# Attention scores in one fp32 product, with the queries read from DRAM onto diagonal blocks

## The chip, the cores and the metric

The kernel runs on one core of one Trainium2 chip. The core has five engines that run side by side and meet through semaphores: TensorE (PE, with its weight load shown apart as PEld), VectorE (DVE), ScalarE (ACT), GpSimd (POOL) and SyncE (SP), which here only issues DMAs. The metric is the device time of one execution in microseconds; lower is better.

## The reference, cut to what matters

A gated linear attention over 768 steps for 4 batches of 8 heads with 40 dimensions feeds a mixture of 8 experts (top 1) and then a dense two-layer network. Only the first part is touched:

```python
for t in range(S):
    m_new = np.maximum(f_gate[:, :, t] + m, i_gate[:, :, t])
    f_stab = np.exp(f_gate[:, :, t] + m - m_new)
    i_stab = np.exp(i_gate[:, :, t] - m_new)
    m = m_new
    C = f_stab * C + i_stab * np.einsum('bhd,bhe->bhde', vt, kt)
    n = f_stab * n + i_stab * kt
    h_tilde = np.einsum('bhde,bhe->bhd', C, qt)
    denom = np.maximum(np.abs(np.einsum('bhd,bhd->bh', n, qt)), 1.0)
    y[:, :, t] = sigmoid(o_gate[:, :, t]) * h_tilde / denom
x = moe(y)          # expert by argmax of x @ w_gate
return ffn(x)       # leaky relu between two dense products
```

## The kernel before

The attention is computed in chunks of 128 steps: 6 chunks, and in each the 32 heads in 11 groups of three (the last has two). One chunk and one group is an **item**; there are 66, and I count them from 1. All of this is the first stage, up to some 228 us; the experts and the dense network come after it and are not changed.

Per item `e_decay` makes the matrix E of gate decays (one product pD of `down` with the gate rows `GM`, then three exponentials on ScalarE). `e_scores` makes pS, the products of 128 keys with 128 queries of each of the three heads: the 120 stacked key rows of the group are the weights, and the queries stand on diagonal blocks of a 120 x 384 tile `qB` whose other blocks are zero, so that one product gives three separate score matrices. VectorE multiplies P = E * pS (L574). `e_out` (L600 to L612) multiplies P, the carried state Cm and the weighted keys kw; `e_kw`, Cm and sums of hA run on POOL.

pS is exact to fp32 by three products of rounded parts: `parts` splits queries and keys of a piece into a high and a low fp32r part (ScalarE casts L539 and L546, VectorE subtracts L542 and L549). A piece is three groups (the last has two), so a chunk has 4 and the stage 24. `blocks` (L333) then copies the rounded queries, high and low side by side, from `qs` in SBUF onto the diagonal blocks of `qB` by three DMAs a piece on SP's queue. There are two `qB` tiles, used in turn.

The order is written out by hand. The loop goes by steps s: step s issues the scores of item s, then the outputs of the item before, and at three points of each step (`small`) whatever a table (`later`) has put there; key 3*s+k is point k of step s. Each engine and SP's queue take their instructions in the order in which they are written. The tables: PART_AT and PO place the splits; GATES the gate sums of chunks 1 to 5; Z0, ZS the 16 writes of zeros (L843) to the rows `xs_d` that are later scattered to the experts; PICK, FR, W1S, TW the first expert's choice, its rows, its weights and the last rows. Short products of a constant tile `rest` (L261) fill known waits of TensorE.

Of the kernel before, what the change touches and what calls it, by code (L numbers as in the profile page):

```python
# [9 lines left out]
F32 = mybir.dt.float32  # L10
# [41 lines left out]
def tile_mlstm_moe_ffn(  # L52
# [189 lines left out]
    with ExitStack() as sx:  # L242
# [37 lines left out]
        QB = [s1.tile([GR, GW, HG, 2, P], F32R, tag=f"qB{i}", name=f"qB{i}") for i in range(2)]  # L280
        for t in QB:
            nc.gpsimd.memset(t.bitcast(F32), 0.0)
# [46 lines left out]
        def blocks(src, dst, p):  # L329
            for j in range(HG):  # L330
                r = slice(D * j, D * j + D)
                nj = sum(HG * g + j < BH for g in range(GCUT[p], GCUT[p + 1]))
                nc.sync.dma_start(dst[r, 0:nj, j].bitcast(F32), src[r, 0:nj].bitcast(F32))  # L333

        def first_loads(p):
            gs = slice(GCUT[p], GCUT[p + 1])
            nc.sync.dma_start(nats["Q", 0][:, gs], qt[0, :, gs])
            nc.sync.dma_start(nats["K", 0][:, gs], kt[0, :, gs])

# [13 lines left out]
        for w in "QKkv":  # L353
            new_nat(w, 0)
# [47 lines left out]
        def gate_steps(c0, c1, eng):  # L402
# [42 lines left out]
            def decays(k):  # L445
# [63 lines left out]
        LD0, LDS, LD1 = 16, 0, -1  # L509
        XO = (11, 14, 2, 10), (7, 14, 0, 10), (9, 14, 1, 10), (7, 10, 4, 9), (9, 14, 1, 10), (6, 10, 0, 11)  # L510
        PART_AT = -15, -8, -8, -4, -5
        PO = 0, 0, 1, 0, 0, 0, 0, 0, 0, 1, 0, 0, 0, 0, 0, 0, 0, 0, 0, 0, 0, 0, 0, 1
        ZC = 2
        Z0, ZS = 24, 1
        TA, TB = 3, 3
        GATES = 1, 3, 8, 9, 10, 11, 12, 18, 20, 22, 23, 25, 27, 28
# [6 lines left out]
        SC0 = 49  # L523
# [3 lines left out]
        def q_blocks(n):  # L527
            c, g = items[n]
            p = piece_of(g)
            return QB[(c * NP + p) % 2][:, g - GCUT[p]]  # L530

        def parts(c, p, k):

            gs = slice(GCUT[p], GCUT[p + 1])
            n = GCUT[p + 1] - GCUT[p]
            kt_, qt_ = (nats[w, c][:, gs] for w in "KQ")
            if k == 0:
                qs = st["qs", c, p] = wk.tile([GR, GW, 2, L], F32R, tag="qs", name=f"qs{c}_{p}")
                nc.scalar.copy(qs[:, :n, 0], qt_)  # L539
            if k == 1:  # L540
                qs = st["qs", c, p]
                nc.vector.tensor_tensor(qs[:, :n, 1], qt_, qs[:, :n, 0].bitcast(F32), ALU.subtract)  # L542
            if k == 2:
                kh, kl = (wk.tile([GR, GW, L], F32R, tag=w, name=f"{w}{c}_{p}") for w in ("kh", "kl"))
                st["k", c, p] = kh, kl
                nc.scalar.copy(kh[:, :n], kt_)  # L546
            if k == 3:
                kh, kl = st["k", c, p]
                nc.vector.tensor_tensor(kl[:, :n], kt_, kh[:, :n].bitcast(F32), ALU.subtract)  # L549
            if k == 4:  # L550
                qs = st.pop(("qs", c, p))
                blocks(qs, QB[(c * NP + p) % 2], p)

# [306 lines left out]
        g_row(0, slice(0, BH))  # L860
        for i in (0, 1, 4, 2, 3):
# [780 lines left out]
```

## Time and profile before

| what | us |
|---|---|
| median of 3 runs (817.66 to 819.74) | 819.6 |
| profiled execution, its own time | 821.43 |
| span of its trace | 819.6 |
| TensorE busy in the span | 754.8 |
| VectorE busy | 503.8 |
| ScalarE busy | 378.0 |
| GpSimd busy | 272.8 |

[...] Matmul records overlap, so the pace of TensorE is read from the distance between starts rather than from durations.

### The profile page before, as it was taken

Reading aid. Unit: us, or ns where it says so; the run is one execution under the profiler, and the core shown is the slowest. Engines: PE = TensorE matmul, PEld = TensorE weight load, DVE = VectorE, ACT = ScalarE, POOL = GpSimd, SP = SyncE. Lnnn points to the kernel's source line nnn. Section 1 sums busy time; section 2 is a strip of 40 time slices with the busy share of each in tenths; the row PEclk is TensorE's granted clock in tenths of the full one; section 3 lists DMA queues with packets and bytes.
Section 4 is the critical chain, followed back from the end, with each engine's and each line's share of the span. In section 5 each row is a group of like instructions: output and inputs, shape, how many; then the busy total and the mean of one; then the engine's idle time right before and its main releaser. Section 6 shows DMA issues by size and latency. Waiting matters only on the chain.

```text
span 819.6 us, 12632 instructions
## 1 busy us (share of the span) xinstructions
PE 754.8 (92%) x4332; PEld 680.9 (83%) x4332; DVE 503.8 (61%) x1097; ACT 378.0 (46%) x842; POOL 272.8 (33%) x434
## 2 busy tenths in 40 slices
PE   5888898897988999989898999999999999999992
PEld 2678898897876788979787999899999999999992
DVE  7485898785576887865866478554443444444330
ACT  5575776463145565544554345433343343343330
POOL 5343776652643355454445332300200200201002
PEclk7899999996799999999898999999999999999996
DMA  5699565633246457777784931100000000000000
GB/s 152 197 330 251 158 212 163 210 116 107 97 135 190 138 177 186 146 195 195 166 198 156 242 124 37 65 1 1 33 1 1 33 1 0 33 1 17 17 1 34
DMA packets 60936, 92.57 MB, mean 113 GB/s; under 512 B 9508, under 2 KB 41508, under 8 KB 60868
## 3 DMA queue, kind: packets, MB, share of 16 engines
q1 hardware_dynamic: 45508, 61.28, 28.0%
q10 hardware_dynamic: 9344, 18.35, 7.2%
q0 software_dynamic: 6016, 12.09, 4.9%
q8 instruction: 36, 0.59, 0.3%
q14 instruction: 32, 0.26, 0.1%
HBM read 63.79 MB, written 19.95 MB: 102 GB/s over the span
## 4 chain that ended last, share of the span: by engine, by line
issue 37%; PE 21%; DVE 15%; DMA 12%; POOL 6%; ACT 4%; SPq 3%; ACTq 0%; POOLq 0%; DVEq 0%
PE pd L1391 7%; PE pu L210 4%; POOL out_dram L93 3%; DMA qB<-qs 3%; DMA w1r<-in_moe_w_dram 2%; DMA wi_d<-d_si 2%; PE pI L606 2%; DMA wo_d<-d_so 2%; SPq L333 2%; DVE w2l L182 1%; PE pe L210 1%; DVE hl L239 1%; DVE lka L1534 1%; DVE P L574 1%; DMA no<-in_o_gate_dram 1%
## 5 line engine op out<-in xcount | busy, mean ns | idle before, releaser
L210 PE MATMUL pva<-xhfa,wi 128*128 128x512 f32 x432 | 134.0, 393 | 0.0
L1534 DVE TENSOR_TENSOR lka<-pva,lka 128x512 f32<-128x512 f32 x96 | 66.2, 690 | 107.6 <-ACT lka L1533 105.7
L93 POOL DMA_INDIRECT out_dram<-ota,meta x24 | 24.0, 1000 | 266.3 <-DVE ota L1510 262.3
L1533 ACT ACTIVATE lka<-pva 128x512 f32<-128x512 f32 x96 | 57.2, 596 | 118.5 <-PE pva L210 110.8
L1539 DVE TENSOR_TENSOR gla<-lka,gha 128x512 fp32r<-128x512 f32 x96 | 68.5, 714 | 63.2 <-ACT gha L1537 62.5
L1537 ACT CAST gha<-lka 128x512 fp32r<-128x512 f32 x96 | 59.6, 621 | 87.1 <-DVE lka L1534 84.1
L210 PEld LDWEIGHTS pva<-xhfa,wi 128*128 128x128 f32 x432 | 78.3, 188 | 12.5
L210 PE MATMUL pu<-xh,w1h 128*128 128x256 f32 (+7 forms) x192 | 66.5, 348 | 6.3 <-DVE hl L239 4.0
L560 ACT ACTIVATE E<-pD,wn 128x128 f32<-128x128 f32 x192 | 56.5, 368 | 30.6 <-PE pD L557 23.4
L1501 PE MATMUL poa<-woaw1h,gla 128*128 128x320 f32 x216 | 66.8, 309 | 0.0
L1500 PE MATMUL poa<-woaw1l,gha 128*128 128x320 f32 x216 | 66.7, 309 | 0.0
L1499 PE MATMUL poa<-woaw1h,gha 128*128 128x320 f32 x216 | 66.6, 308 | 0.0
L210 PE MATMUL pu<-xh,w1l 128*128 128x256 f32 (+7 forms) x192 | 65.7, 344 | 0.0
L606 PE MATMUL pI<-nv,P 128*128 128x123 f32 (+1 forms) x384 | 59.0, 291 | 2.5 <-ACT no L678 1.3
L606 PEld LDWEIGHTS pI<-nv,P 128*128 128x128 f32 x384 | 54.7, 206 | 4.2 <-ACT no L678 1.5
L210 PE MATMUL pva<-xlfa,wi 128*128 128x512 f32 x144 | 56.0, 389 | 0.0
L1391 PE MATMUL pd<-hh,w2l 128*128 128x512 f32 (+6 forms) x128 | 48.2, 377 | 4.8 <-DVE w2l L182 4.4
L1391 PE MATMUL pd<-hh,w2h 128*128 128x512 f32 (+6 forms) x128 | 48.4, 378 | 3.1 <-ACT w2h L181 3.1
L160 POOL TENSOR_TENSOR w1l<-w1r,w1h 128x512 fp32r<-128x512 f32 x19 | 27.1, 1429 | 64.0 <-ACT w1h L159 63.3
L1391 PE MATMUL pd<-hl,w2h 128*128 128x512 f32 (+6 forms) x128 | 47.6, 372 | 0.9 <-DVE hl L239 0.9
L238 ACT ACTIVATE hh<-pu 128x256 fp32r<-128x256 f32 (+7 forms) x64 | 31.7, 501 | 30.7 <-PE pu L210 23.2
L210 PEld LDWEIGHTS pu<-xh,w1h 128*128 128x128 f32 x192 | 36.5, 190 | 9.9 <-DVE hl L239 4.6
(308 smaller groups left out, 2027.5 us busy)
## 6 DMA issues: line engine op xcount, KB each, us to landing
w2r<-in_moe_w_dram SPq DMA_DIRECT2D x16, 640.0 KB
w1r<-in_moe_w_dram SPq DMA_DIRECT2D x16, 512.0 KB
qB<-qs SPq DMA_DIRECT2D x54, 120.0 KB
xs_d<-zr SPq DMA_DIRECT2D x16, 320.0 KB
rdo<-in_moe_w_out_dram ACTq DMA_DIRECT2D x16, 320.0 KB
w1r<-in_moe_w_dram SPq DMA_DIRECT2D x32, 128.0 KB
rdi<-in_moe_w_in_dram ACTq DMA_DIRECT2D x8, 512.0 KB
no<-in_o_gate_dram SPq DMA_DIRECT2D x12, 320.0 KB
```

The lines of the kernel that those rows point to most:

```text
L93: ins = nc.gpsimd.indirect_dma_start(dst, bass.IndirectOffsetOnAxis(ap=idx, axis=0), src, None)
L210: nc.tensor.matmul(ps_t, a, b, start=start, stop=stop)
L560: nc.scalar.activation(Et[:, j], pD[:, j], AF.Exp, bias=wn[:, c, 3, HG * g + j : HG * g + j + 1])
L606: nc.tensor.matmul(pI[:, r0:, j], Pt[:, j], vj, start=True, stop=True)
L1391: nc.tensor.matmul(pd, aa, bb, start=(i == 0), stop=(i == len(seq) - 1))
L1499: nc.tensor.matmul(po[n], g_h[:, tsl], woh, start=(f == 0), stop=False)
L1500: nc.tensor.matmul(po[n], g_h[:, tsl], wol, start=False, stop=False)
L1501: nc.tensor.matmul(po[n], g_l[:, tsl], woh, start=False, stop=(f == NF - 1))
L1533: nc.scalar.activation(lk, pu, AF.Copy, scale=0.01)
L1534: nc.vector.tensor_tensor(lk, pu, lk, ALU.max)
L1537: nc.scalar.copy(g_h, lk)
L1539: nc.vector.tensor_tensor(g_l, lk, g_h.bitcast(F32), ALU.subtract)
```

## The change

The three rounded products become one product of fp32 operands, the keys as loaded (`nK`) against a `qB` of fp32 queries. `parts`, its copies and its subtracts go. `qB` is loaded straight from DRAM by `q_load`, with as many DMAs per piece as before and half the bytes (no low part). There are now 4 `qB` tiles, one for each piece of a chunk, together as large as the two before; the queries of the next chunk go into a tile one step after its last product in this chunk was issued (QL). Chunk 0 no longer loads the plain queries. WARM, the table of filling products, stays.

Around it the order moves: at the start the copy of `down` goes from VectorE to ScalarE, and of the four casts that fill `GM` two go to POOL and none stays on VectorE; the first gate row is sent in two parts; the gate differences of chunks 1 to 5 go from POOL to VectorE, and some of their sums to POOL; the loads of k and v for chunk 1 come earlier; the 16 writes of zeros are put at every second point from step 11 to step 21 instead of every point from step 8 to step 13.

```diff
-        QB = [s1.tile([GR, GW, HG, 2, P], F32R, tag=f"qB{i}", name=f"qB{i}") for i in range(2)]
+        QB = [s1.tile([GR, GW, HG, P], F32, tag=f"qB{i}", name=f"qB{i}") for i in range(NP)]
...
-        def blocks(src, dst, p):
+        def q_load(c, p):
             for j in range(HG):
                 r = slice(D * j, D * j + D)
                 nj = sum(HG * g + j < BH for g in range(GCUT[p], GCUT[p + 1]))
-                nc.sync.dma_start(dst[r, 0:nj, j].bitcast(F32), src[r, 0:nj].bitcast(F32))
+                nc.sync.dma_start(QB[p][r, 0:nj, j], qt[c, r, GCUT[p] : GCUT[p] + nj])
...
-        Z0, ZS = 24, 1
+        Z0, ZS = 33, 2
...
-            kh, kl = (t[:R, g - GCUT[p]] for t in st["k", c, p])
-            nc.tensor.matmul(pS[:, :nh], kh, qB[:R, :nh, 0], start=True, stop=False)
-            nc.tensor.matmul(pS[:, :nh], kh, qB[:R, :nh, 1], start=False, stop=False)
-            nc.tensor.matmul(pS[:, :nh], kl, qB[:R, :nh, 0], start=False, stop=True)
+            nc.tensor.matmul(pS[:, :nh], nats["K", c][:R, g], QB[p][:R, g - GCUT[p], :nh], start=True, stop=True)
...
+        for c in range(1, NC):
+            for p in range(NP):
+                later((3 * ((c - 1) * NG + GCUT[p + 1]) + QL,), q_load, c, p)
```

SP's queue near the start, from the first loads of queries and keys on, before:

```order
L337 DMA nQ_142<-in_qt_dram 120x384
L338 DMA nK_143<-in_kt_dram 120x384
L337 DMA nQ_142<-in_qt_dram 120x384
L338 DMA nK_143<-in_kt_dram 120x384
L386 DMA GM<-gh 1x32x128
L333 DMA qB_134<-qs_0_184 40x3x256 x3
L343 DMA nv_145<-in_v_dram 128x369
L343 DMA nk_144<-in_k_dram 128x360
```

and now:

```order
L338 DMA nK_146<-in_kt_dram 120x384
L334 DMA qB_134<-in_qt_dram 40x3x128 x3
L338 DMA nK_146<-in_kt_dram 120x384
L334 DMA qB_135<-in_qt_dram 40x3x128 x3
L387 DMA GM<-gh 1x18x128
L344 DMA nv_148<-in_v_dram 128x369
L344 DMA nk_147<-in_k_dram 128x360
```

The diagonal blocks of two pieces now stand ahead of the gate row, and nothing that is computed stands ahead of them.

VectorE between the copy of the first turned gates (`wn`) and the first P, before:

```order
L443 COPY wn<-aT_195 128x32
L412 SCALAR_TENSOR_TENSOR g_139<-g_138,g_139 32x640
L429 TENSOR_TENSOR gl_161<-g_139,gh 32x128
L447 TENSOR_TENSOR rst<-g_138,g_139 32x128
L423 SCALAR_TENSOR_TENSOR g_139<-rst,g_138 32x640
L542 TENSOR_TENSOR qs_1_236<-nQ_142,qs_1_236 120x3x128
L574 TENSOR_TENSOR P_266<-E_227,pS_259 128x384
```

and now:

```order
L446 COPY wn<-aT_189 128x32
L415 SCALAR_TENSOR_TENSOR g_143<-g_142,g_143 32x640
L421 TENSOR_TENSOR g_142<-g_142,g_143 32x640
L423 TENSOR_TENSOR g_142<-g_142,g_143 32x640
L432 TENSOR_TENSOR gl_168<-g_143,gh 32x128
L450 TENSOR_TENSOR rst<-g_142,g_143 32x128
L544 TENSOR_TENSOR P_250<-E_220,pS_245 128x384
```

The long second scan (L423 before) has moved behind the first P, and the two differences that it waits for (L421, L423 now) have come from POOL.

SP's queue in the last chunk, from the first expert's weights on, before:

```order
L144 DMA w1r_1_2662<-in_moe_w_dram 128x2x512
L146 ISA
L146 DMA w1r_1_2662<-in_moe_w_dram 64x512
L146 ISA
L146 DMA w1r_1_2662<-in_moe_w_dram 64x512
L333 DMA qB_134<-qs_2_2548 40x3x256 x3
L228 ISA
L228 DMA xr_2798<-xs_d 128x2x320
L333 DMA qB_135<-qs_3_2696 40x2x256 x2
```

and now, a little earlier in the queue:

```order
L334 DMA qB_136<-in_qt_dram 40x3x128 x3
L387 DMA GM<-gh 1x5x128
L334 DMA qB_137<-in_qt_dram 40x2x128 x2
L334 DMA qB_137<-in_qt_dram 40x128
L773 TENSOR_LOAD pick
L773 ISA x2
L774 TENSOR_LOAD pick
L774 ISA x2
L144 ISA
L144 DMA w1r_0_2388<-in_moe_w_dram 128x2x512
```

The last two pieces of queries have moved from behind the weights (`w1r`) to ahead of the choice of the expert (`pick`) on which the weights wait.

## Rows read from the trace of the kernel before

**Rows 1.** Busy time by stretch; columns: stretch, length, busy PE, PEld, DVE, ACT, POOL, clock, DMA share, GB/s.

```profile
0.00:20.20 20.20, 10.08 (x34) 4.86 (x35) 14.74 (x23) 9.98 (x24) 10.61 (x17) 0.79 0.50 150
20.20:48.19 27.99, 24.43 (x160) 20.64 (x159) 14.22 (x33) 15.34 (x49) 10.54 (x35) 0.91 0.76 237
48.19:83.48 35.29, 29.56 (x215) 27.79 (x213) 26.07 (x85) 21.68 (x62) 16.05 (x45) 0.95 0.89 272
83.48:180.77 97.29, 90.04 (x675) 84.98 (x674) 83.08 (x284) 63.64 (x188) 66.51 (x154) 0.98 0.55 170
180.77:208.89 28.12, 23.59 (x118) 22.01 (x116) 17.88 (x60) 10.11 (x30) 8.51 (x9) 0.65 0.38 111
208.89:227.64 18.75, 17.69 (x117) 15.89 (x115) 9.72 (x51) 4.36 (x15) 13.50 (x18) 0.79 0.37 122
```

**Rows 2.** Waits, whole first stage: TensorE on a DMA (total, times, longest).

```profile
PE pS L570 <- DMA qB<-qs: 11.6, 8, 4.0
```

**Rows 3.** Waits of SyncE's DMA queue up to 240 us.

```profile
SPq L333 <- DVE qs L542: 32.3, 14, 4.5
```

**Rows 4.** Timeline of the start: start us, us, engine, line, operation, tiles, idle before.

```profile
1.84 3.97 POOL L282 MEMSET qB<- 120x2304 f32 x2
1.84 4.04 DVE L389 CAST down<-ident 128x128 fp32r<-128x128 f32 x1
...
9.31 0.65 SPq L386 DMA_DIRECT2D GM<-gh  x1
...
10.38 2.59 SPq L333 DMA_DIRECT2D qB<-qs  x3
...
16.43 2.80 DVE L423 TENSOR_TENSOR_SCAN g<-rst,g 32x640 f32<-32x640 f32 x1 [3.05 <-POOL g L420]
...
19.61 0.53 DVE L574 TENSOR_TENSOR P<-E,pS 128x384 f32<-128x384 f32 x1
```

**Rows 5.** Timeline of TensorE, one item at full clock.

```profile
104.74 0.83 PE L606 MATMUL pI<-nv,P 128*128 128x123 f32 x6
105.41 0.39 PE L608 MATMUL pI<-Cm,nQ 120*128 120x123 f32 x2
...
105.76 0.42 PE L570 MATMUL pS<-qB,kh 120*128 120x384 f32 x1
106.03 0.34 PE L571 MATMUL pS<-qB,kh 120*128 120x384 f32 x1
...
106.38 0.33 PE L557 MATMUL pD<-GM,down 128*128 128x384 f32 x1
```

**Rows 6.** Groups by line, 20 to 215 us: busy, mean ns, idle before.

```profile
L549 DVE TENSOR_TENSOR kl<-nK,kh 120x384 fp32r<-120x384 f32 (+1 forms) x23 | 14.3, 623 | 0.0
```

**Rows 7.** Timeline of TensorE at 161 us: a wait on VectorE.

```profile
161.20 0.22 PE L755 MATMUL LR<-oh,ones 128*128 128x24 bf16 x3 [1.89 <-DVE oh L746]
```

**Rows 8.** Busy time by stretch, 2 us each, columns as rows 1.

```profile
68.00:70.00 2.00, 2.00 (x18) 1.96 (x18) 1.38 (x4) 0.00 (x0) 0.70 (x2) 1.00 1.08 229
...
162.00:164.00 2.00, 2.00 (x11) 1.95 (x10) 0.12 (x1) 0.70 (x3) 0.00 (x0) 0.50 0.71 272
```

**Rows 9.** Timeline of TensorE in the last chunk.

```profile
190.00 0.69 PE L570 MATMUL pS<-qB,kh 120*128 120x384 f32 x1 [3.97 <-DMA qB<-qs]
```

**Rows 10.** Timeline of SyncE's DMA queue in the last chunk.

```profile
179.14 0.42 SPq L144 DMA_DIRECT2D w1r<-in_moe_w_dram  x1
...
184.26 2.65 SPq L333 DMA_DIRECT2D qB<-qs  x3
187.38 0.39 SPq L228 DMA_DIRECT2D xr<-xs_d  x1
```

**Rows 11.** Timeline of ScalarE in the last chunk.

```profile
184.62 0.62 ACT L159 CAST w1h<-w1r 128x512 fp32r<-128x512 f32 x1 [1.93 <-DMA w1r<-in_moe_w_dram]
```

**Rows 12.** Busy time by stretch in the last chunk, columns as rows 1.

```profile
190.00:195.00 5.00, 5.00 (x20) 4.90 (x20) 2.50 (x8) 1.72 (x6) 1.85 (x2) 0.50 0.10 33
```

**Rows 13.** DMA issues between 40 and 85 us: count, KB each.

```profile
xs_d<-zr SPq DMA_DIRECT2D x16, 320.0 KB
```

More of the change, by code (lines that the diff above doesn't have):

```diff
@@ L351, in load_rest @@
                     load_nat(nm, 1, hh)
-        for w in "QKkv":
+        for w in "Kkv":
             new_nat(w, 0)
@@ L386, in g_row, with gate_constants @@
             nc.sync.dma_start(GM[0:1, hs].bitcast(F32), gh[hs, c * L : (c + 1) * L].bitcast(F32))
-        def gate_constants():
-            nc.vector.tensor_copy(down, ident)
-            nc.vector.memset(down[0:1].bitcast(F32), 1.0)
+        def gate_constants(k):
+            if k == 0:
+                nc.scalar.copy(down, ident)
+            else:
+                nc.vector.memset(down[0:1].bitcast(F32), 1.0)
         m, G = gates[1][:, 0], gates[1][:, 1]
@@ L522, in tile_mlstm_moe_ffn @@
         SP = 4
-        SC0 = 49
+        SC0 = 67
         TW = 189, 191, 194, 194, 200, 197, 200, 205, 206, 211, 210, 217, 215, 215, 215, 215, 214, 215, 216, 217, 216, 216, 217, 217, 219, 221, 219
         EARLY = 28, 37, 34, 39
[L527 to L552, printed above, removed]
         def e_decay(n):
@@ L859, in tile_mlstm_moe_ffn @@
         g_high()
-        g_row(0, slice(0, BH))
-        for i in (0, 1, 4, 2, 3):
-            parts(0, 0, i)
         a_sum(1)
+        gate_constants(1)
         a_turn(0)
+        g_row(0, slice(0, heads_of(1).stop))
+        mask_rows(2, nc.gpsimd.tensor_copy)
+        mask_rows(3, nc.gpsimd.tensor_copy)
         a_turn(1)
-        later((0,), g_low, nc.vector)
-        first_values(0)
-        first_loads(2)
-        first_values(1)
-        first_loads(3)
-        first_values(2)
-        first_values(3)
-        load_rest()
+        first_values(0)
+        first_values(1)
+        first_loads(2)
+        g_row(0, slice(heads_of(2).start, BH))
+        first_values(2)
+        first_loads(3)
+        first_values(3)
+        later((5,), load_rest)
+        later((0,), g_low, nc.vector)
         later((0,), decays, 0)
@@ L891, in tile_mlstm_moe_ffn @@
             later((t,), *w)
-        for n in range(1, N):
-            c, g = items[n]
-            if g in GCUT:
-                for i, t in enumerate(PART_AT):
-                    later((max(3 * n + t + PO[c * NP + GCUT.index(g)], 0),), parts, c, GCUT.index(g), i)
+        for c in range(1, NC):
+            for p in range(NP):
+                later((3 * ((c - 1) * NG + GCUT[p + 1]) + QL,), q_load, c, p)
         for p in range(NP):
@@ L899, in tile_mlstm_moe_ffn @@
                 later((max(3 * ((c - 1) * NG + GCUT[p + 1]) + GR1, GR0 + p),), g_row, c, heads_of(p))
-        for i, (nm, c, hh) in enumerate([(nm, 1, hh) for hh in range(2) for nm in "kv"] + [("o", c, hh) for c in range(2) for hh in range(2)]):
-            later((LD0 + LDS * i,), load_nat, nm, c, hh)
+        for t, ls in ((6, [(nm, 1, hh) for hh in range(2) for nm in "kv"]), (15, [("o", c, hh) for c in range(2) for hh in range(2)])):
+            for i, ld in enumerate(ls):
+                later((t + i,), load_nat, *ld)
         for i in range(E * ZC):
```

25 lines of the change are left out of this document (10 added, 15 removed).

## Prediction

> **What bounds the kernel now.** I read first the busy time by stretch, with borders at starts of score products: 20.20 (after the first P), 48.19 (product 11, the last of chunk 0), 83.48 (product 22, the last of chunk 1), 180.77 (product 60), 208.89 (product 66), and 227.64, where the experts begin [rows 1]. TensorE is the busiest engine everywhere, but each stretch has idle time and time at a clock below full. At half clock the work takes twice as long, so a mean clock of 0.95 over 35.29 us costs 0.05 * 35.29 = 1.8 us. In this way the five stretches from 20.20 on hold 3.6, 5.7, 7.3, 4.5 and 1.1 us of idle time and 2.5, 1.8, 1.9, 9.8 and 3.9 us of lost clock: 42 us which a stage without waits would not have. Next I read who is waited for: TensorE waited 11.6 us for the DMA that fills qB [rows 2], and that DMA, in SP's queue, waited 32.3 us for VectorE's subtract of the queries [rows 3]. So loaded queries are rounded, copied, and stand in a queue, and what is late there holds TensorE. Two places matter most: the start, where the first P comes at 19.61 us [rows 4], and the last chunk, where one wait of 3.97 us for qB ends at 190.00 [rows 9] and the clock is 0.50 behind it [rows 12], 0.65 in the mean of its stretch [rows 1].
>
> **The change part by part.**
>
> *The score product.* The trace has no fp32 product of 384 columns. Three rounded ones take 106.38 - 105.76 = 0.62 us a block, of which the first takes 106.03 - 105.76 = 0.27, some 0.09 more than its followers [rows 5]. The nearest fp32 rows are P's products: three written products are six instructions, each of 123 columns, and go by at (105.41 - 104.74) / 6 = 0.112 us, 0.91 ns a column [rows 5]. One product of 384 columns is then two instructions of 0.349 us, 0.70 us together, and 0.79 with the first's 0.09. The other end: if an instruction streams its columns as a rounded one does (0.62 / 3 = 0.21), the pair takes 0.41. So the block changes by between -0.21 and +0.17 us. I take 0.75, nearer to the fp32 rows, since part of 0.112 us is a cost per instruction that a wide product pays once: +0.13 us. Every block lies on TensorE, which has no slack once the waits are gone: 60 wide blocks and 6 of two heads (+0.09) make **+8.3 us** (ends -13 and +11).
>
> *The rounded parts.* 24 casts each of queries and keys and 24 subtracts each go; a subtract of keys takes 0.62 us [rows 6]. VectorE loses some 28 us of its work, ScalarE nearly as much. Neither is the bound, so this is no term by itself, but VectorE is busy 83 of 97 us in the long stretch [rows 1], and there TensorE waits for it, as at 161.20, 1.89 us, with the clock at 0.50 behind [rows 7, 8].
>
> *The start, to 20.20 us.* Now the cast of `down` occupies VectorE for 4.04 us beside POOL's two memsets of qB of 3.97 us [rows 4], and the gate chain follows both that and a cast of GM. Both leave VectorE. SP issues two gate loads, two key pieces and six block loads ahead of the gate row: at 0.65 us (the gate row's own) for four and 2.59 / 3 = 0.86 for six that is 7.8 us of issue, and the row, which left at 9.31 [rows 4], leaves near 8.3. So the first decay product comes 1 us earlier, no more. The first P at 19.61 was not held by that but by the scan of 2.80 us that began at 16.43 after a wait of 3.05 us for POOL's differences [rows 4]. That scan stands behind P now. VectorE's row to P is then the other scan and two differences, done by some 12 us, and P waits for pS: three fills and the wide product at half clock behind the third decay product, some 15.2 us. **-4.4 us.** [...]
>
> *Chunk 0, to 48.19.* The pieces of qB are loaded long before their use. Of 3.6 us idle and 2.5 of clock I leave 0.5 for the turn of the gates: **-5.6 us.**
>
> *Chunk 1, to 83.48.* The idle 5.7 us are mostly waits for qB that stood behind other loads. But the 16 writes of zeros, 320 KB each [rows 13], move into this chunk. Of 7.5 us I leave 3.5 for ScalarE's sigmoids and for late transfers: **-4.0 us.**
>
> *Chunks 2 to 5, to 180.77.* Of 7.3 + 1.9 us, waits for VectorE and qB, I leave 4.2: **-5.0 us.** With the price of 38 blocks, 4.9 us, this stretch stays as long as it was.
>
> *The last chunk, to 208.89.* SP's queue issues the first expert's weights from 179.14 on, once the expert is chosen, and two pieces of queries stand behind them: issued from 184.26, used at 190.00 [rows 9, 10]. In the new order the queries are ahead of the choice. The wait goes, 4.0 us, and what followed it: TensorE is 5.00 of 5.00 us busy at 190 to 195, and at 0.50 [rows 12], so the work behind it shrinks with the clock: 9.8 us. What is late next: ScalarE already waits 1.93 us for these weights at 184.62 [rows 11], and the rows `xr`, issued at 187.38 [rows 10], are turned five items after the choice. I put 1.5 us back: **-12.3 us.**
>
> *To 227.64.* 3.9 us of clock; a chain of routing, scatter and load bounds it at the end: **-3.6 us.**
>
> Sum: 8.3 - 4.4 - 5.6 - 4.0 - 5.0 - 12.3 - 3.6 = -26.6 us. Against the profiled execution's own time, 821.4 us (1.8 above its span and above the median), this gives 794.8; I say **795 us**. Experts and dense layers only begin earlier.
>
> **The rivals.**
>
> *A. The clock falls in the last chunk all the same.* With qB's wait gone, TensorE meets the weights or `xr`. After only 1.89 us of idle the clock was at 0.50 [rows 7, 8], and in the last chunk it did not come back while TensorE was fully busy [rows 12]. A wait of some 2 us there brings back the 9.8 us and most of the 3.6: 795 + 12 = 807 us. For it: ScalarE's 1.93 us. Against it: those waits stand beside work, and the wide product leaves fewer gaps.
>
> *B. The DMA engines bound chunk 1.* The zeros (5.2 MB), and by the code's shapes next keys, queries, k, v (2.7 MB), two chunks of output gates (1.3) and blocks (0.7) are 9.9 MB. At 229 GB/s, the rate at a DMA share of 1.08 [rows 8], they take 43 us, where the chunk should take some 33. POOL's first scatter waits for all zeros and holds Cm and kw behind it, TensorE idles and its clock falls: 8 us of the terms of chunks 0 to 2 go and 2 of clock, 805 us. Against it: zeros come last among these loads and only the scatter needs them. [...]
>
> *C. Slower: the wide fp32 product is dearer than the narrow ones say.* Each item's path holds it, 66 times. All gains together are 34.9 us, so it decides from 0.62 + 34.9 / 66 = 1.15 us a block. If each of the two instructions took twice the columns' pace of P's products (1.82 ns), a block would be 1.4 + 0.09 = 1.49 us: 66 * 0.87 - 34.9 = +22, 844 us. P's products at 0.112 us speak against it; only the width, not seen here, speaks for it.
>
> *D. The queries stay late.* A load into qB waits for the last product of that tile, and SP's queue for it. If this takes the place of the old wait, only the start is gained: 821.4 - 4.4 - 3 (for VectorE's freed time) + 8.3 = 822 us. Against it: a whole chunk lies between two uses of a tile.
>
> **How the numbers follow.** Forecast 0.54, A 0.22, B 0.13, C 0.06, D 0.05. The forecast's own range, with its leftovers at nothing (-9.7 us) or doubled and a block at 0.79, is 785 to 807. To hold 8 in 10 I go from 783 to 812, which takes in A, B and some of the low end of the block's price. A change under 0.3% (2.5 us) can't be told from none: D is mostly there, 0.04; C and the rest of D are slower, 0.07; forecast, A and B are faster, 0.89.
>
> **What would show it.** Per step: a score block of two instructions at 0.75 us; the first P near 15 us; product 11 near 39.5 us and product 22 near 72; nearly no wait of TensorE for qB; full clock from 180 us (then near 170) to the experts, which begin near 201. Wrong would be: a block over 0.8 us; a wait over 1.5 us of TensorE for `xr` or for ScalarE in the last chunk with the clock at 0.50 behind (A); POOL's first scatter waiting on the zeros (B); a stretch of chunks 2 to 5 longer than 100 us.

## The result and the profile after

The changed kernel takes 792.05 us (median of 4 runs, 789.86 to 794.8), the kernel before 818.63 beside it: a ratio of 0.9682, 95% interval 0.9641 to 0.9724. Run again beside the last experiments (experiment 12) it gave 790.86 us, beside 821.12 for the kernel before, and 0.9641 (0.9598 to 0.9684). The forecast was 795.0 with 783 to 812, so time and sign came in. The kernel before was 818.63 us beside it, less than the 821.4 that the forecast started from, so the gain is 26.6 us, as forecast to the tenth, and 30.3 us by the second pair of medians. The terms behind it did less well: the start and chunk 1 gained more than was said, chunk 0 and the last chunk with the way to the experts less, and the one cost was four times too high. The profiled execution took 792.8 us, its span is 791.1, the granted clock of TensorE, 1.00 at full speed, 0.974 against 0.953.

First the busy time of the kernel after by stretch, with the same events as borders as in [rows 1]: first P on VectorE, score products 11, 22, 60 and 66, the beginning of the experts (six products that turn `xr`, at 200.60). Columns: stretch, length, then busy time (and instructions) of PE, PEld, DVE, ACT and POOL, granted clock, DMA share, GB/s.

```profile
0.00:12.67 12.67, 9.38 (x28) 4.20 (x28) 9.07 (x17) 5.03 (x9) 11.26 (x19) 0.87 0.58 168
12.67:37.98 25.31, 23.86 (x156) 18.34 (x156) 13.13 (x31) 15.99 (x53) 13.30 (x42) 1.00 0.76 224
37.98:67.00 29.02, 28.73 (x203) 24.47 (x202) 21.22 (x77) 18.30 (x53) 14.15 (x36) 1.00 0.97 326
67.00:160.82 93.82, 90.45 (x637) 78.53 (x636) 70.23 (x252) 54.20 (x160) 64.74 (x152) 1.00 0.52 156
160.82:182.35 21.53, 17.30 (x110) 14.45 (x110) 17.51 (x57) 9.70 (x27) 8.18 (x9) 0.92 0.38 107
182.35:200.60 18.25, 17.18 (x116) 15.54 (x115) 9.61 (x51) 4.27 (x15) 13.26 (x18) 0.81 0.37 127
200.60:791.10 590.50, 559.67 (x3027) 504.86 (x3026) 336.49 (x565) 253.46 (x482) 147.06 (x162) 0.98 0.33 87
```

Length before, length after, and what the prediction had made of the difference (its term with its price of the score blocks in that stretch):

| stretch | before | after | difference | predicted |
|---|---|---|---|---|
| to the first P | 19.61 | 12.67 | -6.9 | -4.4 |
| to product 11 | 28.58 | 25.31 | -3.3 | -4.2 |
| to product 22 | 35.29 | 29.02 | -6.3 | -2.6 |
| to product 60 | 97.29 | 93.82 | -3.5 | -0.1 |
| to product 66 | 28.12 | 21.53 | -6.6 | -11.5 |
| to the experts | 18.75 | 18.25 | -0.5 | -3.6 |
| to the end | 591.96 | 590.50 | -1.5 | 0 |

The middle of the stage is what the forecast wanted: TensorE is 28.73 of 29.02 us busy in chunk 1 and at full clock from 12.67 to 160.82. It no longer waits for qB at all ([rows 2]: 11.6 us), so rival D did not come. The last two stretches are not: the clock is 0.92 and 0.81 there, and 4.2 us of the first of them are idle.

One execution's own start has to be allowed for. Product 11 stands at 37.98 us here, but at 40.25 in the second profile of the same kernel, and at 39.5 to 40.3 in the experiments that leave the start as it is. The clock makes the difference: from the first P to 20.00 us it is 1.00 here and 0.50 in the second profile, where six instructions of P's products take 1.27 us (from 18.43 to 19.70) against 0.67 here (16.44 to 17.11). So chunk 0 gained 3.3 us in this execution and 1.1 in the other (27.46 us). Behind the experts' beginning, which nothing here changes, executions differ too: 590.5 us here, 585.0 in the second profile, and up to 592.6 in the experiments. Differences of lengths inside the stage, from product 11 on, are steadier: the second profile has 29.03, 93.60, 21.98 and 18.63 us where this one has 29.02, 93.82, 21.53 and 18.25.

**The score block.** Timeline of TensorE at full clock (columns: start, duration, engine, line, operation, tiles, count, idle before). First a block and what follows it, then, after the dots, a block that something other than pD follows:

```profile
160.82 0.81 PE L542 MATMUL pS<-qB,nK 120*128 120x384 f32 x2
161.17 0.63 PE L531 MATMUL pD<-GM,down 128*128 128x384 f32 x1
161.64 0.38 PE L570 MATMUL pI<-Cm,nQ 120*128 120x123 f32 x2
161.86 0.80 PE L576 MATMUL pI<-nv,P 128*128 128x82 f32 x6
162.50 0.32 PE L261 MATMUL pS<-rest 128*128 128x384 bf16 x1
162.66 0.81 PE L542 MATMUL pS<-qB,nK 120*128 120x384 f32 x2
...
178.35 0.81 PE L542 MATMUL pS<-qB,nK 120*128 120x384 f32 x2
179.00 0.38 PE L234 MATMUL pt<-ident,xr 128*64 128x128 f32 x2
```

The start of pD, 0.35 us after the block's first instruction, is not the end of the block: the product behind it (L570) starts 0.82 us after the block's start. The same steps took 0.79 before, from 105.76 [rows 5] to the P product behind pD:

```profile
106.55 0.87 PE L606 MATMUL pI<-nv,P 128*128 128x123 f32 x6
```

Where something else than pD follows, as at 178.35, the next start is 179.00: a block takes 0.65 us, as against 0.62.

**The start.** Timeline, all engines:

```profile
1.83 4.05 POOL L283 MEMSET qB<- 120x1152 f32 x4
...
2.92 1.09 SPq L334 DMA_DIRECT2D qB<-in_qt_dram  x3
...
3.54 0.41 DVE L415 TENSOR_TENSOR_SCAN g<-g 32x128 f32<-32x128 f32 x1 [1.62 <-DMA g<-in_i_gate_dram]
...
5.70 0.89 SPq L387 DMA_DIRECT2D GM<-gh  x1
...
10.04 2.10 POOL L436 TENSOR_TENSOR g<-g,g 32x640 f32<-32x640 f32 x1
...
10.67 1.61 DVE L432 TENSOR_TENSOR gl<-g,gh 32x128 f32<-32x128 f32 x1
...
11.14 1.42 PE L542 MATMUL pS<-qB,nK 120*128 120x384 f32 x2
...
12.67 0.55 DVE L544 TENSOR_TENSOR P<-E,pS 128x384 f32<-128x384 f32 x1 [0.19 <-PE pS L542]
```

The first scan (L415, 0.41 us) runs beside POOL's memsets of qB and takes no longer for it: the same scan took 0.40 us in the kernel before, at 7.27 us, with POOL idle. The gate row leaves at 5.70 us, where the prediction had it at 8.3. Its values are ready at 5.57 us, and SP's queue is free by then, since three block loads from DRAM occupy it for 1.09 us, 0.36 each (the copies cost 0.765 to 0.962; the prediction's 0.86 came from them). The wide product comes at 11.14 and the first P at 12.67.

**The last chunk.** Timeline of TensorE:

```profile
169.78 0.80 PE L576 MATMUL pI<-nv,P 128*128 128x82 f32 x6
173.14 0.90 PE L668 MATMUL pX<-ident,x 128*128 128x128 f32 x3 [2.56 <-DVE xl L191]
```
VectorE in the same time:

```profile
169.07 0.66 DVE L612 TENSOR_TENSOR hA<-hA,wn 128x8 f32<-128x8 f32 x1
169.77 0.73 DVE L619 TENSOR_SCALAR den<-hA 128x8 f32<-128x8 f32 x1
170.53 1.19 DVE L623 TENSOR_TENSOR den<-den,hA 128x8 f32<-128x8 f32 x1
```
POOL beside it:

```profile
168.43 1.27 POOL L160 TENSOR_TENSOR w1l<-w1r,w1h 128x512 fp32r<-128x512 f32 x1 [3.34 <-DVE hA L597]
169.66 0.81 POOL L940 TENSOR_TENSOR no<-hA,no 128x320 f32<-128x320 f32 x1
170.43 1.26 POOL L160 TENSOR_TENSOR w1l<-w1r,w1h 128x512 fp32r<-128x512 f32 x1
```
And busy time by stretches of 5 us, columns as above:

```profile
170.00:175.00 5.00, 2.44 (x12) 1.80 (x10) 3.46 (x9) 0.83 (x2) 1.69 (x2) 0.78 0.43 131
175.00:180.00 5.00, 5.00 (x38) 4.32 (x36) 3.74 (x15) 1.98 (x6) 1.50 (x2) 0.88 0.00 0
...
185.00:190.00 5.00, 3.93 (x23) 3.56 (x23) 3.25 (x19) 1.18 (x5) 2.50 (x6) 0.64 0.39 148
190.00:195.00 5.00, 5.00 (x33) 4.81 (x33) 2.27 (x17) 0.15 (x1) 3.07 (x6) 0.67 0.28 102
```

TensorE waits 2.56 us for a bank that VectorE empties (L191). VectorE is late because three instructions on 128 x 8 elements take 0.66, 0.73 and 1.19 us, and each ends 0.03 us after a POOL instruction (169.70, 170.47 and 171.69). The same ones take 0.17 us each at 161.69, 161.90 and 162.44 us, where POOL is idle (161.66 to 163.81). Why these three are held and the scan beside the memsets was not, no row shows. So a wait of the size that rival A asked for did come, with a slow clock behind it, but neither the weights nor `xr` were its cause.

### The profile page after: what moved, and what is told of

Its sections match the earlier page's. It is cut to its first block, busy times and chain, and to the rows that moved or that the text cites. A ratio compares the mean times of both kernels' runs of the same rounds, so it can differ in the third digit from the quotient of the medians.

```text
span 791.1 us, 12320 instructions
## 1 busy us (share of the span) xinstructions
PE 746.6 (94%) x4266; PEld 660.4 (83%) x4266; DVE 477.3 (60%) x1048; ACT 360.9 (46%) x794; POOL 271.9 (34%) x437
## 4 chain that ended last, share of the span: by engine, by line
issue 39%; PE 26%; DVE 15%; POOL 7%; DMA 5%; ACT 4%; SPq 1%; DVEq 0%; POOLq 0%; ACTq 0%
PE pd L1360 7%; PE pu L210 5%; POOL out_dram L93 3%; DMA w1r<-in_moe_w_dram 3%; PE pI L576 3%; PE pS L542 3%; DMA wo_d<-d_so 2%; DVE w2l L182 1%; DVE hl L239 1%; PE pe L210 1%; DVE P L544 1%; DVE lka L1503 1%; PE pD L531 1%; PE LR L692 1%; DMA wi_d<-d_si 1%
## 5 line engine op out<-in xcount | busy, mean ns | idle before, releaser
L576 PEld LDWEIGHTS pI<-nv,P 128*128 128x128 f32 x384 | 50.9, 191 | 5.3 <-DVE P L544 0.9
L576 PE MATMUL pI<-nv,P 128*128 128x123 f32 (+1 forms) x384 | 54.2, 275 | 0.3 <-DVE P L544 0.3
L542 PE MATMUL pS<-qB,nK 120*128 120x384 f32 (+1 forms) x132 | 54.0, 491 | 0.0
```

Source lines behind the costliest of these rows:

```text
L542: nc.tensor.matmul(pS[:, :nh], nats["K", c][:R, g], QB[p][:R, g - GCUT[p], :nh], start=True, stop=True)
L576: nc.tensor.matmul(pI[:, r0:, j], Pt[:, j], vj, start=True, stop=True)
```

## The experiments

Each is timed against the kernel before on the same chip; ratios carry their 95% interval. "After" stands at 0.9682 and 0.9641, so ratios that differ by less than some 0.005 are not told apart.

**1. The product alone (one_product).** In the kernel before:

```diff
-            nc.tensor.matmul(pS[:, :nh], kh, qB[:R, :nh, 0], start=True, stop=False)
-            nc.tensor.matmul(pS[:, :nh], kh, qB[:R, :nh, 1], start=False, stop=False)
-            nc.tensor.matmul(pS[:, :nh], kl, qB[:R, :nh, 0], start=False, stop=True)
+            nc.tensor.matmul(pS[:, :nh], nats["K", c][:R, g], qB[:R, :nh, 0], start=True, stop=True)
```

(with `qB` and `qs` of plain fp32)

> The kernel before with one part of the change alone: the score block is one fp32 product, its queries copied unrounded through the old path, in the old order; the rounding of the keys and the subtract of the queries are left as work whose results nobody reads. Theory P, the prediction's price: a block goes from 0.62 to 0.75 us, 66 blocks make +8.3 us, some of it covered by the old waits for qB: 823 to 827 us. Theory M, from rows of the kernel after (a wide block followed by anything but pD's product takes 0.65 us, from 178.35 to 179.00, and the block with pD behind it 0.82 against 0.79 before): +0.03 us a block, +2 us: 819 to 822 us. Theory S, the starts taken at their word (the next instruction starts 0.35 us after the block's first): -0.27 us a block, -18 us: about 802 us.

820.22 us, ratio 1.0024 (1.0001 to 1.0048): some 2 us slower, theory M. P's 823 would be 1.006 and S's 802 0.980; both lie outside the interval. The order and the waits are still the old ones, as TensorE's waits up to 235 us show (total, times, longest):

```profile
PE pS L569 <- DMA qB<-qs: 10.5, 5, 4.0
```

**2. The product twice (product_twice).** In the kernel after:

```diff
             nc.tensor.matmul(pS[:, :nh], nats["K", c][:R, g], QB[p][:R, g - GCUT[p], :nh], start=True, stop=True)
+            nc.tensor.matmul(pS[:, :nh], nats["K", c][:R, g], QB[p][:R, g - GCUT[p], :nh], start=True, stop=True)
```

> The kernel after with the score product issued twice into the same bank, so that the block is doubled and the result unchanged. What the time grows by is the price of a block where it stands. Theory P (0.75 us a wide block, 60 of them, and 0.53 for 6 narrow ones): +48, 840 us. Theory M (0.65 and 0.44): +41.6, 834 us. Theory S (0.35 and 0.24): +22, 814 us. Where waits hide a part it is less than that by the same share of the 66 blocks; the distance from the first instruction of the first product to that of the second, in the trace, is then the cleaner number.

825.68 us, ratio 1.0089 (1.0056 to 1.0122). From after's two ratios that is 33 to 37 us more, between S and M, and the starts in TensorE's timeline decide:

```profile
167.76 0.81 PE L542 MATMUL pS<-qB,nK 120*128 120x384 f32 x2
168.41 0.81 PE L543 MATMUL pS<-qB,nK 120*128 120x384 f32 x2
```

From the first product to the second it is 0.65 us, and from 171.58 to 172.23 again, as theory M has it; a block of two heads, 256 columns, takes 0.43 (from 43.21 to 43.64). The other 5 to 9 us of theory M's 41.6 are covered: the waits for x (2.4 us) and the last x (1.1) of the kernel after are gone from TensorE's list, 0.3 us are left of the wait for xh (1.4), and 2.1 of its longest. Some four fifths of a block's price show in the total, so TensorE bounds most of the stage.

**3. The queries' loads late (loads_late).** In the kernel after:

```diff
         for c in range(1, NC):
             for p in range(NP):
-                later((3 * ((c - 1) * NG + GCUT[p + 1]) + QL,), q_load, c, p)
+                later((3 * (c * NG + GCUT[p]) - 5 + (1 if (c, p) in ((2, 1), (5, 3)) else 0),), q_load, c, p)
```

> The kernel after with the queries' loads of chunks 1 to 5 back at the old copies' places in the order, five steps ahead of the use; in the last chunk two pieces stand behind the first expert's weights again. Theory O (the place in SP's queue made the wait): TensorE waits 3 to 4 us for qB in the last chunk, with half clock behind it, and 3 to 5 us in all in the other chunks: 792 + 8 to 14 = 800 to 806 us. Theory V (the waits came from the roundings on VectorE and ScalarE that the copy stood behind; a load from DRAM goes out at 0.36 us and is late for nobody): under 1.5 us of wait in the last chunk, 792 to 796 us.

799.47 us, ratio 0.9768 (0.9726 to 0.9810), 7 us above after by the first of its ratios and 10 by the second: nearer to theory O, just under its range. The wait for qB is back in the last chunk, with half clock behind it:

```profile
174.08 1.62 PE L542 MATMUL pS<-qB,nK 120*128 120x384 f32 x2 [2.58 <-DMA qB<-in_qt_dram]
```
The stretches there:

```profile
170.00:175.00 5.00, 1.84 (x10) 1.20 (x9) 2.01 (x6) 0.60 (x2) 0.00 (x0) 0.87 0.76 164
175.00:180.00 5.00, 5.00 (x19) 3.99 (x18) 2.86 (x10) 2.03 (x7) 2.03 (x2) 0.50 0.05 7
```

No other chunk waits for qB, against theory O's 3 to 5 us: a load of 0.34 us of issue (median of 72 in the kernel after; the copies took 0.78) is late here only behind the weights. From product 60 to 66 it is 26.13 us here, 21.53 and 21.98 in the two profiles of after. Chunks 2 to 5 are 2.8 us longer too, at a clock of 0.98 and without a wait for qB; why is open.

**4. The old start (start_old).** In the kernel after, the first stage written in the old order:

```diff
-                nc.scalar.copy(down, ident)
+                nc.vector.tensor_copy(down, ident)
...
-        g_row(0, slice(0, heads_of(1).stop))
-        mask_rows(2, nc.gpsimd.tensor_copy)
-        mask_rows(3, nc.gpsimd.tensor_copy)
+        mask_rows(1, nc.vector.tensor_copy)
+        mask_rows(2)
+        mask_rows(3)
...
-        ... = gate_steps(1, NC, nc.vector)
+        ... = gate_steps(1, NC, nc.gpsimd)
```

> The kernel after with the old order of the first stage alone: down and GM's rows on VectorE, the second scan (chunks 1 to 5) behind POOL's differences, the gate row as one write; the queries are still loaded from DRAM. Theory S (the start is worth what the first P moves, and nothing gives it back): the first P, at 12.67 us after and 19.61 before, comes at 17 to 19.5, and the whole is 4.4 (the prediction's term) to 7 us longer: 796 to 799 us. Theory R (what the start wins, chunk 0 loses by waiting for loads and gates): first P late as well, but product 11, at 37.98 us after, within 2 us of it and the time at 792 to 794 us.

796.04 us, ratio 0.9719 (0.9674 to 0.9764): 3 us above after by the first of its ratios, which is not told apart from it, and 6 by the second. VectorE's timeline shows the old mechanism of [rows 4] again, a scan behind POOL's differences and P behind the scan:

```profile
1.84 2.12 DVE L391 CAST down<-ident 128x128 fp32r<-128x128 f32 x1
...
12.75 2.81 DVE L426 TENSOR_TENSOR_SCAN g<-rst,g 32x640 f32<-32x640 f32 x1 [3.03 <-POOL g L423]
15.49 0.52 DVE L544 TENSOR_TENSOR P<-E,pS 128x384 f32<-128x384 f32 x1
```

The first P stands behind that scan and is later by 2.8 us, but not at 17 to 19.5 as expected: even in the old order it is 4.1 us earlier than before (19.61). Of these, 1.9 us are the cast of `down`, 2.12 us beside four memsets of qB where it took 4.04 beside two of twice the size. Most of the rest came with the roundings, which no longer stand on VectorE ahead of the long scans and of P: in the old order the first P is at 17.47 without them and at 19.61 with them (experiments 8 and 7, both with the queries from DRAM). Product 11 is at 40.61, 0.4 to 1.2 us behind the 39.5 to 40.3 of the other profiles with the new start (2.6 behind the first profile of after), so chunk 0 gives most of the 2.8 us back, as theory R has it. What the total is longer by stands elsewhere: from product 66 to the experts it is 20.86 us at a clock of 0.69, against 18.25 and 18.63 in the two profiles of after; why is open.

**5. The roundings as dead work (parts_dead).** In the kernel after, the casts and subtracts of chunks 1 to 5 put back, their results unread:

```diff
+        for n in range(1, N):
+            c, g = items[n]
+            if g in GCUT and c > 0:
+                for i, t in enumerate((-15, -8, -8, -4)):
+                    later((max(3 * n + t, 0),), parts, c, GCUT.index(g), i)
```

> The kernel after with the roundings of chunks 1 to 5 put back as work that nobody reads: 20 casts each of queries and keys on ScalarE, 20 subtracts each on VectorE, at their old places in the order. Theory W (VectorE and ScalarE have room in the chunks, so their freed time is no term by itself, as the prediction says): 792 to 794 us, TensorE's waits for VectorE as in the kernel after. Theory F (a good part of the gain is VectorE's freed time: 70 of 94 us busy in chunks 2 to 5 of the kernel after, some 20 more by this edit): TensorE waits 3 us or more longer for VectorE's x, P and oh, the clock falls with it, and the time is 796 to 803 us.

798.33 us, ratio 0.9771 (0.9727 to 0.9816): 7 us by the first ratio of after, theory F's time. The prediction had said that the freed time is "no term by itself". TensorE's waits for VectorE grow (x from 2.4 to 3.6 us, oh from 1.1 to 1.5), less than the 3 us that theory F asked for, as the list up to 215 us has it:

```profile
PE pX L686 <- DVE x L662: 3.6, 4, 1.9
```
Chunks 2 to 5 and the last chunk up to product 66, by stretch:

```profile
68.96:164.74 95.78, 90.69 (x637) 78.33 (x635) 83.14 (x284) 63.86 (x188) 67.42 (x154) 1.00 0.50 152
164.74:188.04 23.30, 20.05 (x111) 16.44 (x110) 18.18 (x60) 9.96 (x28) 8.05 (x8) 0.78 0.36 100
```

Chunk 1 is as long as in after (29.05), chunks 2 to 5 are 2.0 us longer, the last chunk 1.3 to 1.8, at a clock of 0.78 instead of 0.92 and 0.84 in the two profiles of after. The profiled execution is the shortest of the four (793.51 us; the others took 798.20 to 802.59), so its rows show only a part of the 7 us.

**6. The zeros and the first scatter at their old places (zeros_old).** In the kernel after:

```diff
-        Z0, ZS = 33, 2
+        Z0, ZS = 24, 1
...
-        SC0 = 67
+        SC0 = 49
```

> The kernel after with the 16 writes of zeros and the first scatter at their old places, ahead of chunk 1 instead of spread over it. In the kernel after chunk 1 moves 326 GB/s at a DMA share of 0.97 and TensorE is 28.7 of 29.0 us busy, so the forecast's rival B (DMA engines bound that chunk) did not come. Theory D (there is room even so): no wait of TensorE for qB, 791 to 794 us. Theory B2 (it is only the spreading that keeps loads in time): the zeros, 5.2 MB, stand ahead of the queries and keys of chunks 1 and 2, TensorE waits 3 us or more for qB or keys, and its clock falls: 796 to 802 us.

793.61 us, ratio 0.9696 (0.9654 to 0.9738): theory D, no wait for qB. Where the zeros stand can't be told from the time.

**7 and 8. The queries from DRAM, in the old order (direct_alone, direct_noparts).** On top of one_product:

```diff
-                nc.sync.dma_start(dst[r, 0:nj, j], src[r, 0:nj])
+                nc.sync.dma_start(dst[r, 0:nj, j, 0], qt[c, r, GCUT[p] : GCUT[p] + nj])
```

and, in direct_noparts, without the casts and subtracts of `parts` too.

> The kernel one_product (the old order, one fp32 product, roundings as work that nobody reads) with one more part of the change: the queries come from DRAM, at the very places in the order where the copies stood. Theory D1 (the copy was late because it stood behind a cast and a subtract, 32.3 us of waiting in SP's queue before): the waits of TensorE for qB fall from 10.5 us to under 4, one of 2 to 4 us staying in the last chunk behind the weights, and the time from 820 to 806 to 813 us. Theory D2 (the place in the order is what counts): 8 us or more of waits stay, 815 to 820 us.

> The kernel direct_alone without the roundings: only the order of the old kernel is left, and the way from here to the kernel after is the order alone. By the runs so far the order is worth 7.4 (loads), 4.0 (first stage) and 1.6 us (zeros), 13 us together, and the roundings some 6. Theory A (the parts add up): 803 to 807 us, and direct_alone 5 to 7 us above it. Theory B (they share the same waits): it comes within 3 us of the kernel after, 790 to 795 us, or direct_alone does not stand above it.

direct_alone 807.71 us, ratio 0.9825 (0.9766 to 0.9884); direct_noparts 805.75 us, ratio 0.9841 (0.9778 to 0.9903). D1's time and waits came: with every place in the order kept, reading the queries from DRAM takes 16 us off one_product (0.9825 against 1.0024), and TensorE's wait for qB, 10.5 us in experiment 1, is in direct_alone (total, times, longest)

```profile
PE pS L568 <- DMA qB<-in_qt_dram: 3.0, 3, 2.4
```

The edit also halves the bytes of these DMAs, and the issue of such a load takes 0.34 us in the kernel after, against 0.78 for a copy in the kernel before (medians of 72), so how much of the 16 us is the wait for cast and subtract and how much the shorter issue is not shown.

What the roundings are worth in the old order the totals can't tell: direct_noparts is 2.0 us below direct_alone by the medians and 1.3 above by the ratios, each with an uncertainty of some 7 us, so theory A's 5 to 7 us and theory B's sign are both possible. The stage tells more, because it leaves out the part behind it, which scatters from 585.0 to 592.6 us. Where it stands at the first P, at the score products 11, 22, 60 and 66, and at the beginning of the experts (us, one execution each):

| kernel | first P | 11 | 22 | 60 | 66 | experts |
|---|---|---|---|---|---|---|
| one_product | 19.60 | 49.21 | 86.10 | 183.19 | 211.07 | 229.32 |
| direct_alone | 19.61 | 45.05 | 75.30 | 172.34 | 198.40 | 216.62 |
| direct_noparts | 17.47 | 44.10 | 73.48 | 167.41 | 191.50 | 211.55 |
| after | 12.67 | 37.98 | 67.00 | 160.82 | 182.35 | 200.60 |
| after, second profile | 12.79 | 40.25 | 69.28 | 162.88 | 184.86 | 203.49 |

Loading from DRAM takes 12.7 us off the stage, 6.6 of them in chunk 1. Without the roundings the stage ends 5.1 us sooner in the old order too: the first P comes 2.1 us earlier, and chunks 2 to 5 take 93.93 us instead of 97.04, although TensorE's wait for qB is 4.2 us there, against 3.0. That is theory A's size. In the new order the same work put back costs 2.9 to 5.8 us of the stage (the experts begin at 206.38 in experiment 5). These are single executions, direct_alone's the longest of its four and direct_noparts' the shortest, so 5.1 us may be too much. But nothing here shows that the freed time of VectorE is worth something in one order only.

**9. Two subtracts off POOL (splits_dve).** In the kernel after (an odd number means POOL):

```diff
-        W1E = 1, 4, -7, 1, 3, 7
+        W1E = 1, 4, 4, 4, 3, 7
```

> The kernel after with the third and fourth subtract of the first expert's weights moved from POOL to VectorE. Theory L: in the last chunk of the kernel after, VectorE's three small instructions at 169.07, 169.77 and 170.53 took 0.66, 0.73 and 1.19 us instead of 0.17 each, each to the end of a POOL instruction beside it, and they lead to the wait of 2.56 us of TensorE at 173.14 with half clock behind it; two of the three POOL instructions gone, VectorE gets some 1.4 us back and pays 1.3 for the two subtracts, of which one lies ahead of the chain: the wait falls to 1 to 2 us, and the clock stays up if it is the shorter: 786 to 791 us. Theory N: VectorE's own work, 4.6 of 5 us busy there, is the chain, and the two subtracts only take POOL's place: 791 to 794 us, the wait again 2 to 3 us.

788.81 us, ratio 0.9647 (0.9612 to 0.9683). The mechanism is confirmed in VectorE's timeline:

```profile
171.56 0.16 DVE L612 TENSOR_TENSOR hA<-hA,wn 128x8 f32<-128x8 f32 x1
171.75 0.17 DVE L619 TENSOR_SCALAR den<-hA 128x8 f32<-128x8 f32 x1
171.96 0.17 DVE L623 TENSOR_TENSOR den<-den,hA 128x8 f32<-128x8 f32 x1
```
And in TensorE's:

```profile
170.37 0.41 PE L234 MATMUL pt<-ident,xr 128*128 128x128 f32 x2 [0.44 <-DMA xr<-xs_d]
...
173.55 0.90 PE L668 MATMUL pX<-ident,x 128*128 128x128 f32 x3 [1.06 <-DVE xl L191]
```

The three instructions take 0.16 to 0.17 us again, and the wait falls from 2.56 us (2.40 in the second profile of after) to 1.06 us. The gain is not confirmed: the ratio can't be told from after's, and the stretch from product 60 to 66 is 21.96 us, as long as in after. Behind a wait of 0.44 us for `xr` and the 1.06 us that are left of this one, the clock is at 0.50 all the same, as the stretches show:

```profile
170.00:175.00 5.00, 3.57 (x22) 3.10 (x22) 4.43 (x15) 2.16 (x6) 1.03 (x1) 0.79 0.49 136
175.00:180.00 5.00, 5.00 (x27) 4.29 (x26) 2.25 (x7) 1.43 (x5) 1.27 (x1) 0.50 0.00 0
```

**10. The waits filled (tail_fill).** In the kernel after:

```diff
-            (x_trans, c, 1),
+            (lambda: (keep_warm(16), x_trans(c, 1)),),
...
-            (x_trans, c, 2),
+            (lambda: (keep_warm(8), x_trans(c, 2)),),
...
-            (x_trans, c, b, 0, 2),
+            (lambda: (keep_warm(6), x_trans(c, b, 0, 2)),),
```

> The kernel after with products of no use to the result (16, 8 and 6 of 384 columns) put on TensorE ahead of the three transposes in the last chunk for which it waits 2.56, 1.43 and 1.07 us. Theory C (the price of these waits is the clock behind them, 0.78 and 0.88 at 170 to 180, 0.64 and 0.67 at 185 to 195: some 5 us lost): the waits stay in the clock's eyes filled, the clock stays at 1.00 in the last chunk, and the time falls by 3 to 5 us: 787 to 789 us. Theory L (what is late there is VectorE's chain, and TensorE's slow stretch lies in its shadow): full clock as well, but the experts begin no sooner than 200 us and the time is 791 to 793 us.

789.47 us, ratio 0.9649 (0.9613 to 0.9685). The clock stays up, from product 60 to 66 and on to the experts:

```profile
162.30:183.26 20.96, 19.79 (x134) 15.36 (x134) 18.09 (x57) 9.75 (x27) 8.17 (x9) 1.00 0.41 111
183.26:199.08 15.82, 15.62 (x122) 13.26 (x120) 9.68 (x51) 4.33 (x15) 13.20 (x18) 1.00 0.43 146
```

From product 60 to the experts it is 20.96 + 15.82 = 36.8 us, against 39.8 and 40.6 in the two profiles of after: 3.0 to 3.8 us less in the stage, as theory C has it. In the total this does not show beyond the scatter: by the ratios it is 2.7 us less than the first measurement of after and 0.7 more than the second. The 30 filling products are in those 36.8 us. At 162.66 - 162.50 = 0.16 us each, from the rows on the score block, they are 4.8 us, so an estimate for the two stretches without the filled waits and without the fill is 32.0 us; the prediction had them at 31.8 (28.1 - 11.5 and 18.75 - 3.6).

**11 and 12. Both edits together, and after once more (fill_splits, after_again).** fill_splits has the edits of experiments 9 and 10.

> The kernel after with the edits of tail_fill and splits_dve together. Theory A: the fill keeps the clock at 1.00 and the two subtracts on VectorE end the blocking beside POOL, so the wait at the first transpose is 1 us instead of 2.5 and costs no clock: 2 us less than tail_fill alone, 786 to 788 us. Theory B: with 16 filling products in the way (2.6 us of TensorE's time whether it would wait or not) the shorter chain is not seen: 788 to 790 us.

> The kernel after, unchanged, beside the others of this call: 792 us, ratio 0.968 to the kernel before, as a measure for fill_splits, of which theory A says 4 to 6 us less and theory B 2 to 4 us less.

790.16 us, ratio 0.9637 (0.9591 to 0.9683), and 790.86 us, ratio 0.9641 (0.9598 to 0.9684). Theory B: the shorter chain is not seen. Beside after on the same chip 0.7 us are left of the gain by the medians, inside the scatter and less than theory B allowed. None of the three variants is shown to beat the kernel after.

## Why the prediction came out right, point by point

**The score block: mis-sized, +8.3 us said, about +2 measured.** Two wide instructions take 0.65 us together (experiment 2), where 0.75 was taken, and the product alone costs 2 us (experiment 1), 0.03 us a block times 66. Half of the 0.10 us is the pace read from P's products, 0.91 ns a column: two wide instructions go by at 0.84 to 0.85 (0.65 us for 768 columns, 0.43 for the 512 of a block of two heads). The rows of after show what a narrow instruction pays beside its columns: six of 82 columns go by from 161.86 to 162.50, 0.107 us each, a third fewer columns than P's 123 for nearly the same time as their 0.112; a least price per instruction of about that is an estimate from these two widths. The other half is the step from 0.70 towards 0.79, a surcharge of the first rounded product that the wide fp32 block does not show. Rival C is gone with it.

**The start: right in its mechanism, too small.** The first P comes 6.9 us earlier instead of 4.4: 2.8 for the new order, in which the scan no longer stands ahead of it, 1.9 for the shorter cast of `down`, and the rest for the most part for the roundings that stood on VectorE (experiment 4). The mis-sized step is SP's issue ahead of the gate row, 0.36 us a block load instead of 0.86. Chunk 0 then gained 3.3 where 4.2 were given, and 1.1 in the second profile. Up to product 11 the two terms together were 8.6 us, and 10.2 and 7.9 came: what the start won beyond its term, chunk 0 gave back in the second profile, at half clock up to 20 us. POOL's work beside VectorE does hold something at the start: L432, on 32 x 128, takes 1.61 us beside POOL's L436 (0.25 in experiment 4). But P waits for pS then (12.67, 0.19 us), so it costs nothing.

**Chunk 1 and rival B: the ceiling was wrong.** The 229 GB/s that the prediction took as the rate at a full DMA share was what those transfers moved, not a limit. A stretch of 5 us in chunk 1 of the kernel after:

```profile
55.00:60.00 5.00, 5.00 (x37) 4.49 (x38) 2.27 (x7) 2.31 (x8) 1.87 (x5) 1.00 1.04 391
```
And the first scatter, in POOL's timeline:

```profile
69.51 1.23 POOL L93 DMA_INDIRECT xs_d<-x,dsti  x1 [0.58 <-DVE x L644]
```

At a share of 1.04 the engines moved 391 GB/s. The first scatter waits 0.58 us, for VectorE and not for zeros. Chunk 1 gained 6.3 us where 2.6 were given: of the 3.5 us left for sigmoids and late transfers some 1 was needed (-7.5 + 0.3 for the blocks + 0.9 = -6.3), and most of the gain is there with the queries from DRAM alone (30.25 us in direct_alone, 36.89 in one_product).

**Chunks 2 to 5: right but for the price of the block.** -5.0 was given and 4.9 taken back for 38 blocks; with 0.03 us a block it would have been -5.0 + 1.1 = -3.9, and -3.5 came. That the freed VectorE is "no term by itself" is not what the profiles show: putting its work back costs 2.0 us of these chunks in the new order, and taking it away saves 3.1 in the old one (experiments 5, 7 and 8). The -5.0 us held some of this as waits for VectorE.

**The last chunk and the way to the experts: the largest miss, -15.1 said, -7.1 measured.** The step "what is late next" named the weights and `xr` and put 1.5 us back, without clock. The weights' wait is 0.39 us; what was late was VectorE, held beside POOL. Rival A had the right consequence (a wait near 2 us and the clock behind it) with the wrong cause, and the two stretches came 8.0 us short, where rival A gave 12. That the old place makes a wait for qB is shown by experiment 3 (2.58 us, 7 us in all), that POOL makes some 1.5 us of the new one by experiment 9, and that full clock is worth 3 to 4 us of this stretch by experiment 10.

**The sum.** Up to product 60 the kernel gained 20.0 us (17.9 in the second profile) where 11.3 were said, some 6 of the difference being the block's price; on the last two stretches it gained 8.0 less (8.8). The errors cancelled, and that 795 lies within 3 us of the median is luck to that extent. What stays open: which edit brings the 13 to 16 us between direct_noparts and after. By the table in experiments 7 and 8 the stage is 8.1 to 11.0 us shorter, 3.9 to 6.1 of it before product 11, 0.5 to 0.7 in chunks 1 to 5, and 3.5 to 4.4 behind product 60. Undone one at a time from after, the loads' places, the start and the zeros cost 7, 3 and 1 us by the first ratio of after, with uncertainties of some 5 us each; only the first is told apart from nothing.

## What to carry to other kernels

Price an instruction by one of its own width: a pace read from narrow ones may hold a least price per instruction (82 columns took 0.107 us here, 123 took 0.112), and two widths of the same kind in the trace tell whether it does. When a wait goes, look for what is late next on every engine that feeds the waiting one, and for instructions that take several times their usual duration beside another engine (1.19 us instead of 0.17 here): such a row names the next wait. An engine that is not the bound can be worth time when it is freed (7 us in experiment 5), so give it a term. Where the part behind the change scatters more than the effect, compare the stages in the traces before the totals.

## What the runs showed of the hardware

- A score product of 384 columns in fp32 is two instructions and takes 0.65 us at full clock; three fp32r products of the same size took 0.62. The printed start of pD behind it, 0.35 us after the block's first instruction, is not the block's end: the product behind pD starts 0.82 us after it, pD's own 0.17 us (106.38 to 106.55 before) included.
- Three blocks read from DRAM cost SP's queue 1.09 us, 0.34 each in the median of 72; copies from SBUF, the same places written, 0.78 each (median of 72 in the kernel before).
- An fp32 instruction of 384 columns takes 0.325 us at full clock and one of 256 columns 0.215 (experiment 2), one of 123 columns 0.112 [rows 5] and one of 82 columns 0.107.
- VectorE's instructions on 128 x 8 elements take 0.17 us with POOL idle (161.69 to 162.61 in the kernel after) and up to 1.19 beside POOL's subtract of 128 x 512, ending 0.03 us after it.
- At a DMA share of 1.04 the engines moved 391 GB/s in chunk 1 of the kernel after; at 1.08 they had moved 229 before [rows 8].
- With waits of 0.44 and 1.06 us between 170 and 175 us, the granted clock was 0.50 from 175 to 180 us (experiment 9); with the waits filled it stayed at 1.00 (experiment 10).
- At a clock of 0.50 TensorE's products took 1.8 to 1.9 times as long as at 1.00, where the prediction reckons twice: three rounded products 1.12 us (190.00 [rows 9] to 191.12, clock [rows 12]) against 0.62 [rows 5], six of 82 columns 1.15 us (191.85 to 193.00) against 0.64 (161.86 to 162.50 in the kernel after), six of 123 columns 1.27 in the second profile of after against 0.67 in the first. For time at 0.50 its lost clock is by that some 5 to 10 per cent too high. Timeline of TensorE in the kernel before:

```profile
191.12 0.52 PE L557 MATMUL pD<-GM,down 128*128 128x384 f32 x1
...
191.85 1.42 PE L606 MATMUL pI<-nv,P 128*128 128x82 f32 x6
193.00 0.67 PE L570 MATMUL pS<-qB,kh 120*128 120x384 f32 x1
```
